# Attention and two token mixers on one core: the exponentials turned chunk by chunk, the value products of a pair issued together, and a planner with other prices

## The chip, the core and the metric

The kernel runs on one core of a Trainium2 chip. The metric is device time in microseconds (us) of one execution, the median of several runs. TensorE (PE in the profile) multiplies matrices, VectorE (DVE), ScalarE (ACT) and GpSimd (POOL) work on elements, and the queue of SyncE (SP) issues the transfers.

## The reference, cut to what matters

```
q_n, k_n = rmsnorm(q, g_q), rmsnorm(k, g_k)        # q, k, v: 4 x 12 heads x 448 x 64
scores = scale * q_n @ k_n^T ; scores -= max       # 448 x 448 for each head
attn = exp(scores) / (sum + 1e-9)
x = concat(attn @ v)                               # 4 x 448 x 768
h = relu(x @ w_in); u, v = halves of h             # first mixer (gated over tokens)
x = (u * (w_spatial @ norm(v) + b)) @ w_out
u = x + (relu(x^T @ w_tok1) @ w_tok2)^T            # second mixer, over tokens
out = u + relu(u @ w_ch1) @ w_ch2                  # and over channels
```

## The kernel before

48 heads are worked as 24 pairs; a pair's two heads lie side by side on the 128 partitions. The first eight pairs (`WHOLE`) multiply queries and keys in plain fp32; later ones split each operand into two fp32r parts and make three passes. Up to pair 9 (`AFTER`) the division by the softmax sum follows the value product; from pair 10 on POOL scales the exponentials first (`normalise`).

A pair's 448 queries are four chunks of 112. For a chunk, `scores` makes two score tiles (one for each head, both at once in half the array's rows each: 64 rows by 128 columns), DVE takes the negated row maxima (`nm`), and ACT the exponentials (`e`, 112 x 896 for both heads, ring of six). The value product needs the exponentials with the keys on the partitions, so `turned` transposes them on PE into PSUM (`tp`) and ACT or DVE copies them out (`et`). There are seven key tiles to a pair. Before, `turned(i, n)` takes one key tile out of all four chunks: four transposes of 112 columns and one copy of 128 x 448, into a ring of six `et` tiles. Five of seven copies are ACT's and two (`ON_DVE`) are DVE's. `values(i, kc)` multiplies one of four groups of keys with the values, the two heads in half the array's columns each (128 rows by 64 columns), and accumulates in one bank (`av`).

`slot(s)` writes the work of pair s's scores among the turning and the value products of pair s - 1, and `merge` weaves that with the first mixer (`moe`, one generator for each batch of six pairs) and the conversion of the weights. None of that is the final order. Every operation goes into a `Plan`: `estimate` gives it a price in ns, and `place` simulates the engines by list scheduling, eight rounds backward and forward, and keeps the shortest. Three of its parts matter here. An operation is marked by `op.parts` if it uses half of the array; the plan adds `SWITCH` ns to a matmul whose mark differs from that of the one before, and looks among what is ready (within `NEAR`) for work of the same mark first. Half-array matmuls that belong together are joined and stay next to each other. A pool's ring (`bufs`) makes the first writer of a buffer wait for all users of the tile that held it. `sync` (SP) is an engine of the plan like the others, so the order of the transfers comes out of it too.

The program after the first mixer (second mixer over tokens, then over channels, a Strassen form) is planned by the same code and has no half-array work.

Of the kernel before, what the change touches and what calls it, by code (L numbers as in the profile page):

```python
# [149 lines left out]
class Plan:  # L150
# [8 lines left out]
    def add(self, engine, fn, args, kwargs):  # L159
# [17 lines left out]
        op.parts = engine == "tensor" and fn == "matmul" and (ins[0].shape[0] <= 64 or out.shape[0] <= 64)  # L177
# [9 lines left out]
        for x in ins:  # L187
            t = x.tile
            assert t.writers, "read before it is written"
            op.deps.update(w for y, w in t.writers if x.meets(y))  # L190
# [23 lines left out]
    def estimate(self, engine, fn, out, ins, kwargs):  # L214
# [4 lines left out]
        if engine == "tensor":  # L219
# [27 lines left out]
    def fence(self, pools, act):  # L247

        op = Op()
        op.engine, op.call, op.cost, op.late, op.more, op.parts = "fence", act, 0, 0, [], False  # L250
# [12 lines left out]
    def place(self, before, after, lag, weight, tiles=None):  # L263
# [9 lines left out]
        parts, port = False, 0.0  # L273
# [151 lines left out]
SWITCH, NEAR = 75, 2500  # L425
# [6 lines left out]
TO = {"tensor": 100, "scalar": 0, "vector": 0, "gpsimd": 28, "sync": 0, "fence": 0}  # L432

# [17 lines left out]
def attention_moe_mixer(  # L451
# [150 lines left out]
    class Attention:  # L602
# [88 lines left out]
        def scores(self, i, c):  # L691
# [3 lines left out]
            if c == 0:  # L695
                self.sums[i] = p.tile([P, 2 * C], F32, tag="sum", bufs=3, name="sums")
            sums, qt, kt = self.sums[i], self.qt[i], self.kt[i]
            nm = p.tile([P, 2], F32, tag="nm", bufs=4, name="nm")
            e = p.tile([T, 2, S], F32, tag="e", bufs=6, name="e")
            sc = [psum.tile([P, 512], "sc", "sc")[:T, :S] for _ in range(2)]  # L700
            cs = slice(c * T, (c + 1) * T)
            with nc.joined_up():
                for n, (x, w) in enumerate(PASSES[:1] if i < WHOLE else PASSES):
                    for r in range(2):
                        me = slice(r * D, (r + 1) * D)
                        if i < WHOLE:
                            nc.tensor.matmul(sc[r], qt[me, cs], kt[me], start=True, stop=True)
                        else:
                            nc.tensor.matmul(
                                sc[r], qt[me, x, cs], kt[me, w], start=n == 0, stop=n == len(PASSES) - 1)  # L710
            for r in range(2):
                nc.vector.reduce_max(nm[:T, r:r + 1], sc[r], axis=AX.X, negate=True)
            for r in range(2):
                at = 2 * c + r
                nc.scalar.activation(
                    e[:, r], sc[r], AF.Exp, bias=nm[:T, r:r + 1], scale=1.0, accum_out=sums[:T, at:at + 1])
            self.e[i, c] = e
# [31 lines left out]
        def turned(self, i, n):  # L749
# [10 lines left out]
            tpf = tp.rearrange("p c t -> p (c t)")  # L760
            if n in ON_DVE:
                nc.vector.tensor_copy(et, tpf)
            else:
                nc.scalar.activation(et, tpf, AF.Copy)

        def values(self, i, kc):
# [4 lines left out]
            if kc == 0:  # L771
# [674 lines left out]
```

## Time and profile before

| | |
|---|---|
| time, median of 3 runs (range) | 909.92 us (909.79 to 911.64) |
| the profiled execution's own time; its span | 912.7 us; 910.2 us |
| mean granted TensorE clock | 0.996 |
| busy: PE, DVE, ACT, POOL | 872.9 (96%), 691.1 (76%), 532.3 (58%), 421.5 (46%) us |
| instructions: PE, DVE, ACT, POOL | 5134, 1335, 1267, 533 |
| chain that ended last, share of the span | PE 78%, DVE 7%, ACT 6%, DMA 4%, issue 2% |

Busy time is the time in which an engine had work by the profile, and the share is of the span. The time of an execution is 2.5 us over its span here. The attention with the first mixer takes about the first half of the span. All operations have one line in the profile (that of the recording layer), so groups are told apart by the names of their tiles. A matmul of plain fp32 with half of the array leaves two records in the trace, so a `values` group (two instructions in the order) is four records, and so is a `scores` chunk of the first eight pairs; a chunk of a later pair is six instructions and six records.

### The profile page before, as it was taken

The page shows a single profiled execution, that of the slowest core. Times are in us where ns is not written, and L with a number is a line of the kernel's source. Part 1 is how long each engine was busy: PE and PEld are TensorE (multiplying, and loading weights), DVE is VectorE, ACT ScalarE, POOL GpSimd, SP SyncE. Part 2 cuts the span into 40 slices and gives each one's busy share as a digit, 9 for nine tenths or more (in the row PEclk, how much of TensorE's full clock was granted, in tenths as well). Part 3 has the DMA queues.
Part 4 walks back from the last instruction along what each step waited for, and adds up shares of the span by engine and source line. Part 5 has one row for each costly group of instructions (what it writes and reads, how often), then busy time and mean ns, then how long its engine had stood idle before and what let it go on. Part 6 is the DMA issues. An engine that isn't in the chain of part 4 may idle for free.

```text
span 910.2 us, 15803 instructions
## 1 busy us (share of the span) xinstructions
PE 872.9 (96%) x5134; PEld 713.2 (78%) x5134; DVE 691.1 (76%) x1335; ACT 532.3 (58%) x1267; POOL 421.5 (46%) x533
## 2 busy tenths in 40 slices
PE   3889999999999999999999999999999999999998
PEld 1444476777677677767888999988898999999998
DVE  4799889776786766887555336777799997899973
ACT  5998987777776766776443446645325655333331
POOL 2665655776576555455224313466600307334550
PEclk9999999999999999999999999999999999999999
DMA  6555655566534666344678657766563874661441
GB/s 155 152 140 155 192 141 140 157 209 176 169 88 123 175 192 188 83 132 126 199 250 266 206 160 248 264 175 198 154 179 90 245 225 153 198 191 47 137 156 62
DMA packets 149106, 152.30 MB, mean 167 GB/s; under 512 B 77856, under 2 KB 130656, under 8 KB 147488
## 3 DMA queue, kind: packets, MB, share of 16 engines
q1 hardware_dynamic: 149024, 151.29, 56.1%
q8 instruction: 41, 0.67, 0.3%
q14 instruction: 41, 0.34, 0.1%
HBM read 112.44 MB, written 38.80 MB: 166 GB/s over the span
## 4 chain that ended last, share of the span: by engine, by line
PE 78%; DVE 7%; ACT 6%; DMA 4%; issue 2%; SPq 1%; POOL 1%; ACTq 0%; DVEq 0%; POOLq 0%
PE o_ps L418 15%; PE h2ps L418 15%; PE tp L418 8%; PE av L418 6%; PE ups L418 6%; PE vps L418 6%; PE sc L418 5%; PE xps L418 5%; PE sps L418 4%; ACT e L418 3%; PE u_ps L418 3%; PE h1ps L418 3%; SPq L418 1%; DVE word L418 1%; DMA c_d<-word 1%
## 5 line engine op out<-in xcount | busy, mean ns | idle before, releaser
L418 PE MATMUL h2ps<-op,w 128*128 128x448 f32 x756 | 157.6, 369 | 1.0 <-DVE c L418 1.0
L418 PE MATMUL o_ps<-w,op 128*128 128x384 f32 x882 | 154.0, 335 | 2.7 <-ACT w L418 1.4
L418 PEld LDWEIGHTS o_ps<-w,op 128*128 128x128 f32 x882 | 152.8, 188 | 3.8 <-ACT w L418 1.7
L418 PEld LDWEIGHTS h2ps<-op,w 128*128 128x128 f32 x756 | 142.3, 189 | 15.1 <-DVE c L418 2.4
L418 ACT ACTIVATE e<-sc,nm 112x448 f32<-112x448 f32 x192 | 120.5, 636 | 36.5 <-DVE nm L418 18.9
L418 DVE TENSOR_REDUCE nm<-sc 112x1 f32<-112x448 f32 x192 | 110.3, 616 | 16.6 <-PE sc L418 15.8
L418 POOL TENSOR_TENSOR src<-src 128x384 f32<-128x384 f32 x48 | 61.3, 1288 | 102.3 <-DMA src<-c_d 94.8
L418 PE MATMUL tp<-ident,e 112*128 112x112 f32 x672 | 95.0, 262 | 5.0 <-ACT et L418 2.2
L418 PEld LDWEIGHTS tp<-ident,e 112*128 112x128 f32 x672 | 74.3, 140 | 25.6 <-ACT et L418 7.0
L418 ACT ACTIVATE op<-c 128x768 fp32r<-128x768 f32 x49 | 41.5, 847 | 84.8 <-PE o_ps L418 67.8
L418 POOL TENSOR_SCALAR e<-e,sums 112x448 f32<-112x448 f32 x112 | 71.9, 658 | 38.6 <-DVE sums L418 14.5
L418 ACT ACTIVATE et<-tp 128x448 f32<-128x448 f32 x120 | 65.1, 550 | 22.2 <-PE tp L418 19.9
L418 DVE TENSOR_SCALAR word<-word 128x256 uint32<-128x256 uint32 (+5 forms) x132 | 58.2, 456 | 25.7 <-ACT word L418 24.6
L418 DVE SCALAR_TENSOR_TENSOR word<-raw,word 128x256 uint32<-128x256 uint32 (+2 forms) x132 | 74.1, 567 | 1.1
L418 PE MATMUL ups<-xp,wu 128*128 128x448 f32 x288 | 70.4, 379 | 0.0
L418 POOL TENSOR_TENSOR u<-u,o 128x384 f32<-128x384 f32 x28 | 41.1, 1480 | 62.9 <-ACT o L418 34.2
L418 PE MATMUL av<-et,v 128*64 128x448 f32 x288 | 65.9, 557 | 0.1
L418 DVE TENSOR_TENSOR op<-c,op 128x768 fp32r<-128x768 f32 x49 | 57.6, 1176 | 9.5 <-ACT op L418 9.3
L418 PE MATMUL xps<-wo,g 128*128 128x256 f32 x432 | 62.2, 290 | 1.2 <-DVE sums L418 0.8
L418 DVE TENSOR_TENSOR w<-src,w 128x384 fp32r<-128x384 f32 x84 | 60.0, 737 | 3.4 <-ACT w L418 3.4
L418 DVE TENSOR_TENSOR c<-c,h2ps 128x448 f32<-128x448 f32 x84 | 49.7, 616 | 14.0 <-PE h2ps L418 13.7
L418 PEld LDWEIGHTS xps<-wo,g 128*128 128x128 f32 x432 | 55.1, 190 | 6.6 <-issue 1.3
(120 smaller groups left out, 1653.5 us busy)
## 6 DMA issues: line engine op xcount, KB each, us to landing
src<-c_d SPq DMA_DIRECT2D x132, 192.0 KB, 2.8
wu<-wu_d SPq DMA_DIRECT2D x16, 768.0 KB, 4.8
wo<-wo_d SPq DMA_DIRECT2D x12, 1024.0 KB, 5.1
raw<-in_moe_w_ch_dram SPq DMA_DIRECT2D x36, 256.0 KB, 3.4
raw<-in_moe_w_ch_dram SPq DMA_DIRECT2D x24, 384.0 KB, 3.8
raw<-in_q_dram SPq DMA_DIRECT2D x48, 112.0 KB, 3.0
u<-u_d SPq DMA_DIRECT2D x28, 192.0 KB, 3.8
out_dram<-u SPq DMA_DIRECT2D x28, 192.0 KB, 2.1
```

The lines of the kernel that those rows point to most:

```text
L418: getattr(getattr(self.nc, op.engine), fn)(*args, **kwargs)
```

## The change

`turned(i, c)` now takes one chunk through all seven key tiles: seven transposes into two PSUM tiles (four and three), and two copies, 128 x 4 x 112 and 128 x 3 x 112, into one `et` tile for the pair (`bufs=1`). DVE copies the smaller half of chunks 1 and 3. `values(i)` issues the four groups of a pair in one call. In `slot`, chunks 0 and 1 of pair s are turned within its own slot, chunks 2 and 3 in the next, and `normalise(s, 2)` stands at the slot's end. The ring of `e` goes from six to five. In the planner half-array work has two marks (1: half the rows; 2: half the columns), `SWITCH` goes from 75 to 200 ns, and the prices of half-array matmuls are lower. `covered` only checks that a tile is written before it is read.

```diff
-        op.parts = engine == "tensor" and fn == "matmul" and (ins[0].shape[0] <= 64 or out.shape[0] <= 64)
+        op.parts = 0
+        if engine == "tensor" and fn == "matmul":
+            op.parts = 1 if ins[0].shape[0] <= 64 else 2 if out.shape[0] <= 64 else 0
...
-                return 0.326 * n if ins[0].shape[0] <= 64 else n / 2.4 + 13, 200
-            if ins[0].shape[0] <= 64:
-                return 1.04 * n, 200
-            return n / 1.2 + 54 if out.shape[0] <= 64 else n / 0.6, 200
+                return 0.223 * n if ins[0].shape[0] <= 64 else n / 2.4 + 15, 200
+            return 0.838 * n if min(ins[0].shape[0], out.shape[0]) <= 64 else n / 0.6, 200
...
-SWITCH, NEAR = 75, 2500
+SWITCH, NEAR = 200, 2500
...
-        def turned(self, i, n):
+        def turned(self, i, c):
...
-            r, kc = n % 2, n // 2
-            t = kc * P + r * (S + R)
-            tp = psum.tile([P, C, T], "tp", "tp")
-            for c in range(C):
-                nc.tensor.transpose(
-                    tp[:, c, :], self.e[i, c].rearrange("p r k -> p (r k)")[:, t:t + P], ident[:T, :T])
-            et = self.et[i, n] = self.p.tile([P, S], F32, tag="et", bufs=6, name="et")
+            if c == 0:
+                self.et[i] = self.p.tile([P, ET, S], F32, tag="et", bufs=1, name="et")
+            e = self.e[i, c].rearrange("p r k -> p (r k)")
+            for h, tiles in enumerate((range(C), range(C, ET))):
+                tp = psum.tile([P, C, T], "tp", "tp")
+                for n in tiles:
+                    t = n // 2 * P + n % 2 * (S + R)
+                    nc.tensor.transpose(tp[:, n - tiles[0], :], e[:, t:t + P], ident[:T, :T])
+                et = self.et[i][:, tiles[0]:tiles[-1] + 1, c * T:(c + 1) * T]
+                tpf = tp[:, :len(tiles)]
+                if (c, h) in ON_DVE:
+                    nc.vector.tensor_copy(et, tpf)
+                else:
+                    nc.scalar.activation(et, tpf, AF.Copy)
...
-        def values(self, i, kc):
+        def values(self, i):
...
+            for kc in range(C):
+                with nc.joined_up():
+                    for r in range(2):
...
-    ON_DVE = (3, 5)
-    SLOT = 10
-    PREP0, LAG, SPAN = 1, 0.5, 6
+    ET, EB = 2 * C - 1, 5
+    ON_DVE = (1, 1), (3, 1)
+    SLOT = 8
+    TWO = 99
+    PREP0, LAG, SPAN = 1, 0.2, 5.8
```

The statements of `slot` in their new order:

```
load(s+2) load_v(s) scale(s+1) scores(s,0) | turned(s-1,2) | turned(s-1,3) transposed(s+1,0) |
scores(s,1) normalise(s,0) transposed(s+1,1) values(s-1) | scores(s,2) | turned(s,0) norms(s+2) |
turned(s,1) | scores(s,3) normalise(s,2)
```

What the plan makes of it differs on every engine nearly from the start; only the last 1,627 of PE's instructions (the channel mixer, but for its first few matmuls) stand as before. Three places follow.

PE around the value product of pair 14 (its values' tile is v_3435 before and v_3437 after; `sc` are score matmuls, `av` the value product, `sps` and `ups` the first mixer's). Before:

```order
L418 MATMUL sc<-kt,qt 112x448 x6
L418 MATMUL av<-et,v_3435 64x448 x2
L418 MATMUL sps<-ws,vn 128x448 x3
L418 MATMUL tp<-ident,e 128x112 x7
L418 MATMUL sps<-ws,vn 128x448 x4
L418 MATMUL tp<-ident,e 128x112
L418 MATMUL sps<-ws,vn 128x448
L418 MATMUL tp<-ident,e 128x112 x3
L418 MATMUL sps<-ws,vn 128x448
L418 MATMUL tp<-ident,e 128x112
L418 MATMUL av<-et,v_3435 64x448 x4
L418 MATMUL av<-et,vrest 64x448 x2
```

After, PE for the same pair:

```order
L419 MATMUL sc<-kt,qt 112x448 x12
L419 MATMUL ups<-xp,wu 128x448
L419 MATMUL av<-et,v_3437 64x448 x6
L419 MATMUL av<-et,vrest 64x448 x2
L419 MATMUL sc<-kt,qt 112x448 x12
L419 MATMUL sps<-ws,vn 128x448 x2
L419 MATMUL tp<-ident,e 128x112 x7
L419 MATMUL sps<-ws,vn 128x448 x8
L419 MATMUL tp<-ident,e 128x112 x7
```

The four groups of the value product stand in one piece, score chunks by twos, and a chunk's seven transposes together.

SP's queue at the start (`raw` are the queries and keys of pairs 0 and 1, `g` the two gain vectors, loaded by four transfers). Before, from its sixth row on:

```order
L418 DMA g<-in_g_q_dram 64x1
L418 DMA g<-in_g_k_dram 64x1
L418 DMA g<-in_g_q_dram 64x1
L418 DMA raw<-in_q_dram 112x4x64 x2
L418 DMA raw<-in_k_dram 112x4x64
L418 DMA g<-in_g_k_dram 64x1
L418 DMA raw<-in_k_dram 64x64
L418 DMA raw<-in_k_dram 112x3x64
L418 DMA raw<-in_k_dram 48x64
```

After, SP from the same place:

```order
L419 DMA raw<-in_q_dram 112x4x64 x2
L419 DMA raw<-in_k_dram 112x4x64
L419 DMA raw<-in_k_dram 64x64
L419 DMA raw<-in_k_dram 112x3x64
L419 DMA raw<-in_k_dram 48x64
L419 DMA g<-in_g_q_dram 64x1
L419 DMA g<-in_g_k_dram 64x1
L419 DMA g<-in_g_q_dram 64x1
L419 DMA g<-in_g_k_dram 64x1
```

The last gain transfer stands behind three more transfers than before.

ACT at the start (`whole` are the transposed queries and keys of a pair, `e` its exponentials, `word` and `wpart` weights that are converted). Before, from the copies of pair 0 to those of pair 1:

```order
L418 ACTIVATE whole<-tp,gg 128x448
L418 ACTIVATE word<-raw 128x512
L418 ACTIVATE ry<-ra 112x16
L418 ACTIVATE ry<-ry 112x16
L418 ACTIVATE e,sums<-sc,nm 112x448 x4
L418 ACTIVATE word<-raw 128x512
L418 ACTIVATE sq<-raw 112x512
L418 ACTIVATE e,sums<-sc,nm 112x448 x2
L418 ACTIVATE sq<-raw 112x512
L418 ACTIVATE e,sums<-sc,nm 112x448 x2
L418 ACTIVATE whole<-tp 128x448
L418 ACTIVATE whole<-tp,gg 128x448
```

After, ACT over the same stretch and on to the first copies of `et`:

```order
L419 ACTIVATE whole<-tp,gg 128x448
L419 ACTIVATE word<-raw 128x512 x2
L419 ACTIVATE e,sums<-sc,nm 112x448 x4
L419 ACTIVATE whole<-tp 128x448
L419 ACTIVATE whole<-tp,gg 128x448
L419 ACTIVATE e,sums<-sc,nm 112x448 x4
L419 ACTIVATE et<-tp 128x4x112
L419 ACTIVATE et<-tp 128x3x112
```

Pair 1's copies stand four exponentials earlier, and pair 0's first chunk is copied out right behind its exponentials.

## Rows read from the trace of the kernel before

**Rows 1.** Windows: stretch, length, each engine's busy us (instructions), PE clock, DMA share, GB/s.

```profile
50.00:100.00 50.00, 44.93 (x271) 21.85 (x268) 45.50 (x96) 46.25 (x129) 29.11 (x42) 1.00 0.53 148
130.00:480.00 350.00, 346.90 (x2211) 257.57 (x2210) 257.42 (x615) 235.81 (x638) 192.57 (x303) 1.00 0.55 160
```

**Rows 2.** Timeline of PE, 184 to 201 us: start, time, operation, records.

```profile
184.04 2.39 PE L418 MATMUL sps<-ws,vn 128*128 128x448 f32 x11
186.27 0.55 PE L418 MATMUL tp<-ident,e 112*128 112x112 f32 x4
...
187.58 1.47 PE L418 MATMUL sc<-kt,qt 64*112 64x448 f32 x12
188.98 0.88 PE L418 MATMUL ups<-xp,wu 128*128 128x448 f32 x3
...
192.77 0.55 PE L418 MATMUL tp<-ident,e 112*128 112x112 f32 x4
193.25 0.97 PE L418 MATMUL av<-et,v 128*64 128x448 f32 x4
194.15 0.47 PE L418 MATMUL sps<-ws,vn 128*128 128x448 f32 x1
194.46 0.45 PE L418 MATMUL tp<-ident,e 112*128 112x112 f32 x3
...
197.67 0.93 PE L418 MATMUL tp<-ident,e 112*128 112x112 f32 x8
198.53 1.72 PE L418 MATMUL av<-et,v 128*64 128x448 f32 x8
200.19 0.86 PE L418 MATMUL sc<-kt,qt 64*112 64x448 f32 x6
200.97 0.97 PE L418 MATMUL av<-et,vrest 128*64 128x448 f32 x4
```

**Rows 3.** ACT's groups by form: busy us, mean ns of one, idle before.

```profile
L418 ACT ACTIVATE et<-tp 128x448 f32<-128x448 f32 x120 | 65.1, 550 | 22.2 <-PE tp L418 19.9 <-PE av L418 1.9
...
L418 ACT ACTIVATE ws<-tp 128x336 fp32r<-128x336 f32 x4 | 1.9, 464 | 0.7 <-PE tp L418 0.7
```

**Rows 4.** DVE's groups by form.

```profile
L418 DVE TENSOR_REDUCE nm<-sc 112x1 f32<-112x448 f32 x192 | 110.3, 616 | 16.6 <-PE sc L418 15.8
...
L418 DVE COPY et<-tp 128x448 f32<-128x448 f32 x48 | 29.8, 621 | 21.1 <-PE tp L418 20.9
...
L418 DVE TENSOR_TENSOR ws<-tp,ws 128x336 fp32r<-128x336 f32 x4 | 2.0, 492 | 0.0
```

**Rows 5.** Timeline of SP's queue, 7 to 10 us: start, issue time, transfer.

```profile
7.48 0.50 SPq L418 DMA_DIRECT2D g<-in_g_k_dram  x1
8.02 1.74 SPq L418 DMA_DIRECT2D raw<-in_k_dram  x3
```

**Rows 6.** Timeline of DVE at the start; in brackets the idle time before and its releaser.

```profile
9.84 0.27 DVE L418 TENSOR_TENSOR gg<-g 128x1 f32<-128x1 f32 x1 [2.85 <-DMA g<-in_g_k_dram]
...
10.23 0.69 DVE L418 TENSOR_TENSOR raw<-raw,ry 112x512 f32<-112x512 f32 x1
```

**Rows 7.** Timeline of PE at the start.

```profile
10.97 1.75 PE L418 MATMUL tp<-ident,raw 112*128 112x112 f32 x8 [10.97 <-DVE raw L418]
...
19.43 1.01 PE L418 MATMUL sc<-whole 64*112 64x448 f32 x4
24.26 3.20 PE L418 MATMUL sc<-whole 64*112 64x448 f32 x8 [3.82 <-ACT whole L418]
```

**Rows 8.** Windows around PE's pause in the third ten microseconds.

```profile
20.60:24.20 3.60, 0.00 (x0) 0.00 (x0) 3.56 (x9) 3.60 (x13) 0.73 (x2) 0.94 0.75 176
24.20:27.50 3.30, 3.24 (x9) 1.19 (x10) 1.16 (x3) 2.60 (x10) 2.35 (x6) 0.55 0.46 122
```

**Rows 9.** POOL's groups by form.

```profile
L418 POOL TENSOR_SCALAR e<-e,sums 112x448 f32<-112x448 f32 x112 | 71.9, 658 | 38.6 <-DVE sums L418 14.5 <-ACT sq L418 8.5 <-PE sc L418 4.9
```

More of the change, by code (lines that the diff above doesn't have):

```diff
@@ L189, in add @@
             assert t.writers, "read before it is written"
+            assert t.make or covered(x, t.writers), "read before all of it is written"
             op.deps.update(w for y, w in t.writers if x.meets(y))
@@ L249, in fence @@
         op = Op()
-        op.engine, op.call, op.cost, op.late, op.more, op.parts = "fence", act, 0, 0, [], False
+        op.engine, op.call, op.cost, op.late, op.more, op.parts = "fence", act, 0, 0, [], 0
         op.port = False
@@ L272, in place @@
         start = [0.0] * len(ops)
[L273 removed]
+        parts, port = 0, 0.0
         bank = {}
@@ L432, with covered, volume @@
 TO = {"tensor": 100, "scalar": 0, "vector": 0, "gpsimd": 28, "sync": 0, "fence": 0}
+def covered(x, writers):
+    left = volume(x.box)
+    for y, _ in writers:
+        left -= volume([(max(a, c), min(b, d)) for (a, b), (c, d) in zip(x.box, y.box)])
+    return left <= 0
+def volume(box):
+    n = 1
+    for a, b in box:
+        n *= max(0, b - a)
+    return n
 def free(shape):
@@ L689, in transposed, with scores @@
                 self.raw.pop(i), self.r.pop(i)
-        def scores(self, i, c):
+        def scores(self, i, *cs):
             if not 0 <= i < NP:
@@ L694, in scores @@
             p = self.p
-            if c == 0:
+            if cs[0] == 0:
                 self.sums[i] = p.tile([P, 2 * C], F32, tag="sum", bufs=3, name="sums")
             sums, qt, kt = self.sums[i], self.qt[i], self.kt[i]
[L698 to L701, printed above, removed]
+            scs = {c: [psum.tile([P, 512], "sc", "sc")[:T, :S] for _ in range(2)] for c in cs}
@@ L702, in scores @@
             with nc.joined_up():
[L703 to L717, printed above, removed]
+                for c in cs:
+                    sc, at0 = scs[c], slice(c * T, (c + 1) * T)
+                    for n, (x, w) in enumerate(PASSES[:1] if i < WHOLE else PASSES):
+                        for r in range(2):
+                            me = slice(r * D, (r + 1) * D)
+                            if i < WHOLE:
+                                nc.tensor.matmul(sc[r], qt[me, at0], kt[me], start=True, stop=True)
+                            else:
+                                nc.tensor.matmul(
+                                    sc[r], qt[me, x, at0], kt[me, w], start=n == 0, stop=n == len(PASSES) - 1)
@@ new lines, in scores @@
+            for c in cs:
+                nm = p.tile([P, 2], F32, tag="nm", bufs=4, name="nm")
+                e = self.e[i, c] = p.tile([T, 2, S], F32, tag="e", bufs=EB, name="e")
+                for r in range(2):
+                    nc.vector.reduce_max(nm[:T, r:r + 1], scs[c][r], axis=AX.X, negate=True)
+                for r in range(2):
+                    at = 2 * c + r
+                    nc.scalar.activation(
+                        e[:, r], scs[c][r], AF.Exp, bias=nm[:T, r:r + 1], scale=1.0, accum_out=sums[:T, at:at + 1])
@@ L770, in values @@
             b, j = divmod(i, KD)
[L771 to L773 removed]
+            av = mm_tile("av")
             v32, rest = self.v32[i]
[L775 to L782 removed]
+            for kc in range(C):
+                with nc.joined_up():
+                    for r in range(2):
+                        lhs = v32[:, r, kc] if kc < C - 1 else rest[:, r]
+                        rhs = self.et[i][:, 2 * kc + r if kc < C - 1 else 2 * kc]
+                        nc.tensor.matmul(
+                            av[r * D:(r + 1) * D, :S], lhs, rhs, start=kc == 0, stop=kc == C - 1)
             at = i % XB
@@ L830, in slot @@
             yield
-            self.turned(s - 1, 0)
-            self.turned(s - 1, 1)
+            self.turned(s - 1, 2)
             yield
-            self.values(s - 1, 0)
+            self.turned(s - 1, 3)
             self.transposed(s + 1, 0)
```

37 lines of the change are left out of this document (8 added, 29 removed).

## The prediction

> **What bounds the kernel now.** I read the page's busy shares first, then windows by stage, then PE's timeline, then what ACT, DVE and SP do at the start. From 130 to 480 us, the stretch in which attention and the first mixer run together, PE is busy 346.90 of 350 us at full clock while ACT has 236 and DVE 257 [rows 1]: there the time is PE's own, and a microsecond less of PE work is a microsecond less of span. From 50 to 100 us, where only attention and the conversion of weights run, PE, DVE and ACT are all near 90% (44.9, 45.5 and 46.3 of 50) [rows 1]: a triangle in which a saving on one engine need not show. Behind 480 us nothing of the change is left but what the plan shuffles; the last 1,627 matmuls keep their order, and I count that part at nothing (half a microsecond either way).
>
> **What a visit to half of the array costs.** PE's timeline gives the price of each step as the distance between starts [rows 2]. One group of the value product (four records) takes 0.90 us until the next operation starts (193.25 to 194.15), two groups 1.66 (198.53 to 200.19): 0.76 a group and 0.14 for a visit. A score chunk (six records) takes 0.78 (200.19 to 200.97), two chunks 1.40 (187.58 to 188.98): 0.62 a chunk and 0.16 a visit. The neighbours pay too. Eight transposes ahead of a value product take 0.86, four take 0.48: 0.095 each, so four should take 0.38 and the passage into the half array adds 0.10. The first full-array matmul behind the value product takes 0.31 (194.15 to 194.46) where eleven take 2.23, or 0.20 each (184.04 to 186.27): 0.11 for the passage out. I use 0.105 for either.
>
> **The sum on PE.** The multiplications stay the same in number and shape: as many transposes, score and value matmuls. What changes is how often PE goes from one form to another. Counted along the two orders, stretches of value products go from 60 to 32 (24 pairs, so before a pair's four groups came in two or three pieces), stretches of score chunks from 71 to 58, and passages between half and full array, both directions together, from 144 to 150, since score and value stretches that used to lean on each other are now more often apart. 28 x 0.14 = 3.9 less, 13 x 0.16 = 2.1 less, 6 x 0.105 = 0.6 more: 5.4 us less. Of the changes of form, 66 become 58 up to the value product of the sixth pair, and 137 become 107 behind it, so some nine tenths of the saving lie where PE sets the time.
>
> The Trainium skill (TensorEngine Tiling (Array Packing), Key Properties) says that changing the tiling mode, and not just the tile, drains TensorE, so by it every one of the 203 changes of form before, 165 after, would cost alike. At the mean of the rows' costs (60 x 0.14 + 71 x 0.16 + 144 x 0.105 = 34.9 us over 203, 0.17 each) the sum by that rule would be 38 x 0.17 = 6.5 us, one more than by the rows; the trace agrees that the direct passage from scores to values costs too, which the old plan took for none.
>
> **Copies out of PSUM.** A pair had seven copies of 448 columns, five on ACT at 550 ns [rows 3] and two on DVE at 621 [rows 4]. It gets four of 448 and two of 336 on ACT, two of 336 on DVE. The trace has 336 columns out of PSUM at 464 ns on ACT [rows 3] and at 492 on DVE (a subtraction, not a copy) [rows 4]. ACT: 4 x 550 + 2 x 464 - 5 x 550 = 378 ns more a pair; DVE: 2 x 492 - 2 x 621 = 258 less. Behind 130 us both engines have a fourth of their time free, so this hides. In the first eight pairs ACT gains 3.0 us of work and DVE loses 2.1. Bounds: 0 if the balance of the three engines takes it up, 3.0 if ACT alone sets the pace. I take 1.0, the net of both, being nearest to a stage in which they are equally full.
>
> **The start.** DVE begins pair 0's scaling only behind the product of the gains, which waits for the fourth gain transfer until 9.84 [rows 6]; PE's first work waits for that scaling at 10.97 [rows 7]. The fourth gain was issued at 7.48, and three issues of keys took 1.74 behind it [rows 5]. Now those three stand ahead of it, and DVE's queue still has the product ahead of the scaling: 1.7 us later, for PE and everything after it. Against it: pair 1's copies out of PSUM stood behind eight exponentials and now behind four. Before, PE paused 3.82 us for them at 20.4 and came back slow: eight records of scores took 3.20 us at 24.26, where four had taken 1.01 [rows 7], because the granted clock was 0.55 of full there (near the lower of its two levels) [rows 8]. In the pause ACT was busy 3.60 of 3.60 and DVE 3.56 [rows 8], so the pause itself was covered; what was lost is the slow stretch behind it, 3.20 - 2.02 = 1.2, and ACT's and DVE's idle time in it (0.7 and 2.1 of 3.3) [rows 8]. Bounds for the whole start: 1.7 slower if nothing is won back, 2.5 faster if the slow stretch goes and the idle time of ACT and DVE is used. I take 1.0 faster than without it for the slow stretch, so 0.7 slower, and 0.9 us of saved passages in the early stage is not counted at full. Start, copies and that stage come to about 1 us slower, and what mixer work comes earlier to fill PE's pauses (the first mixer's first matmul stands 7 us of PE work earlier in the order, into a stage that is a tenth idle: 0.7) brings it to nothing. I count the first 130 us at 0, bounds -5 and +5.
>
> **The sum.** The profiled execution took 912.7 us (span 910.2), 2.8 over the median of 909.92. 912.7 - 5.4 + 0 = 907.3; as a median 904.5.
>
> **New waits.** The pair's one `et` tile makes a pair's first copy wait for the last value matmul of the pair before; behind that copy in ACT's queue stand exponentials and other copies. In PE's order the next transposes come behind the value product nearly everywhere, so the wait is mostly over by then. The ring of five `e` tiles holds one chunk back until four chunks earlier is turned, which is long done. From pair 10 on, the chunk's turning waits for POOL's scaling: two maxima at 616 ns [rows 4] for each of two chunks, the exponentials, then two or four scalings at 658 ns [rows 9]. Before, the first two chunks of a pair had plenty of PE work in between (8 us at least, counted at the prices above) and the last two some 5; now both have from 5 up. PE waited little for either before (346.90 busy of 350), so I take 0 with a bound of 0.5 a pair, 7 us for 14 pairs.
>
> **Rivals.**
> First, faster than that: turning a chunk right behind its exponentials shortens the way through the first six pairs. PE idles 5.07 of 50 us in that stage [rows 1], 9.4 over the 92 us from 21 to 113; if half of it goes, 4.7 us more: 899.8. For it: chunks no longer wait for the pair's fourth exponential. Against: ACT has 92% of its time full there and gets more.
> Second, no change: the scaling on POOL arrives late at both halves of a pair. 14 pairs at 0.35 us are 4.9, and 909.4 is left. For it: the two halves are now equally tight. Against: the last two chunks were as tight before, and PE hardly waited.
> Third, slower: the one `et` tile stops ACT. A whole value product takes 0.14 + 4 x 0.76 = 3.2 us, and if ACT stands for a third of it (1.1) in each of the first eight pairs, where nothing makes up for it, that is 8.5; with 1.7 at the start and 1.0 of copies, less 5.4, 5.8 us more: 915.7. It decides from 0.35 us a pair on. Against it is the order: copies stand behind value products.
> That the plan would not bring the groups together is ruled out by the order itself.
>
> **How the numbers follow.** The forecast has 0.56, its own range 900.5 to 908.5; the faster case 0.19; no change 0.12; slower 0.13. About 0.2% (1.8 us) is what a measurement of this kernel tells from no change: faster means below 908.1, slower above 911.7. The forecast gives 0.53 faster and 0.03 same; the faster case all of its 0.19; the second 0.02, 0.09 and 0.01; the third all slower but for 0.01. Together 0.74, 0.13, 0.13. The range goes from 897 (start at its good bound on top of most of the first rival) to 911.5, leaving out most of the slow case.
>
> **What would show it.** Right: from 130 us on PE's busy time stays at its level while the first mixer ends some 5 us earlier; a value product of four groups takes about 3.2 us in one piece; the copies take about 465 ns for 336 columns on ACT; PE's first transposes start at about 12.6. Wrong: `av` or `et` as releaser of ACT's waits by more than 3 us in the first 120 us; PE waiting for POOL's `e` in several pairs; the stage behind 600 us longer by more than a microsecond; or a visit whose cost did not go although the stretches were joined.

## The result, and the profile after

The changed kernel takes 900.49 us (median of four runs, 898.39 to 902.25) against 909.96 for the kernel before on the same chip: 0.9877 of its time, 95% interval 0.9854 to 0.9900. The profiled execution took 900.49 us against 912.7, its span 898.7 against 910.2. Forecast were 904.5: the direction was right and the time lay in the range, but a gain of 5.4 us was forecast, and 9.5 (by the medians) to 12.2 (by the profiled executions) were measured. The gain was mis-sized by about a factor of two.

Windows of the changed kernel, columns as in [rows 1]; the first two answer to [rows 8], the next two to [rows 1]:

```profile
20.60:24.20 3.60, 3.40 (x22) 1.63 (x20) 3.60 (x8) 3.31 (x11) 0.00 (x0) 1.00 0.64 162
24.20:27.50 3.30, 2.11 (x17) 1.46 (x15) 3.30 (x9) 3.30 (x9) 1.84 (x2) 1.00 0.47 118
50.00:100.00 50.00, 44.67 (x273) 23.90 (x269) 42.72 (x100) 47.49 (x136) 35.53 (x50) 0.97 0.57 161
130.00:480.00 350.00, 344.90 (x2239) 265.03 (x2239) 254.36 (x633) 243.98 (x666) 198.85 (x304) 1.00 0.59 174
```

Where PE stood idle for 3.60 us it now works 3.40, and the granted clock stays at 1.00, the higher level. The lower level comes once later instead: from 53.8 to 57.2 us, behind a pause of 0.96 us (the 0.97 of the third row). From 130 to 480 us PE is busy 2.0 us less than before (344.90 of 350 against 346.90) and still starts 2,239 records where it started 2,211: more work in the same stretch. The stage that changed most is in neither row. Windows from 100 to 130 us, first of the kernel before:

```profile
100.00:130.00 30.00, 28.64 (x167) 16.73 (x166) 25.86 (x62) 25.33 (x74) 17.05 (x27) 1.00 0.59 161
```

The changed kernel:

```profile
100.00:130.00 30.00, 30.00 (x175) 19.66 (x173) 25.08 (x63) 25.11 (x70) 17.92 (x28) 1.00 0.54 150
```

**How the gain is placed.** Busy time hides the cost of passages, so I counted useful work: each matmul that starts before a time t, at the distance of its starts in long undisturbed runs of its form (0.203 us for `ups` and `sps`, 0.096 for a transpose, 0.755 for a `values` group). The sum for the changed kernel less that for the one before is its lead at t: -1.1 us at 20, +1.2 at 30, +2.0 at 100, +5.6 at 130, +10.8 at 480, +11.4 at 850. So 5.6 us come from the first 130 us, 5.2 from the next 350, and 0.6 from the rest. This splits the 11.5 us between the spans of the two profiled executions; the medians lie 9.5 apart, so some 2 us of it is scatter between executions.

**The sixth pair** shows what happens before 130 us. The first mixer's products take the value products of six pairs: its first few matmuls can run on the pairs that are done, but no product is complete before the sixth. PE's timeline (start, time, operation, records), score and value products of that pair and the mixer's first matmul, in the kernel before:

```profile
84.29 1.01 PE L418 MATMUL sc<-whole 64*112 64x448 f32 x4
...
98.38 0.97 PE L418 MATMUL av<-et,v 128*64 128x448 f32 x4
...
105.33 1.01 PE L418 MATMUL av<-et,v 128*64 128x448 f32 x4
...
109.03 0.97 PE L418 MATMUL av<-et,vrest 128*64 128x448 f32 x4
...
115.63 0.73 PE L418 MATMUL vps<-wv,xp 128*128 128x512 f32 x2
```

The same in the changed kernel, with the first rows of the start, which answer to [rows 7]:

```profile
12.29 1.75 PE L419 MATMUL tp<-ident,raw 112*128 112x112 f32 x8 [12.29 <-DVE raw L419]
14.81 3.33 PE L419 MATMUL sc<-whole 64*112 64x448 f32 x8 [0.76 <-ACT whole L419]
...
20.79 1.01 PE L419 MATMUL sc<-whole 64*112 64x448 f32 x4
21.73 0.89 PE L419 MATMUL tp<-ident,e 112*128 112x112 f32 x7
22.82 1.76 PE L419 MATMUL sc<-whole 64*112 64x448 f32 x8 [0.20 <-ACT e L419]
...
82.25 1.01 PE L419 MATMUL sc<-whole 64*112 64x448 f32 x4
...
100.03 2.48 PE L419 MATMUL av<-et,v 128*64 128x448 f32 x12
102.33 0.92 PE L419 MATMUL av<-et,vrest 128*64 128x448 f32 x4
103.94 1.40 PE L419 MATMUL vps<-wv,xp 128*128 128x512 f32 x5
```

The last score chunk of the sixth pair comes 2.0 us earlier, its last value group 6.7 earlier, the mixer's first matmul 11.7 earlier. From last score chunk to last value group (starts; I call it the lag) it was 24.7 us and is 20.1; the mean over the first six pairs fell from 21.7 to 17.4.

The start answers to [rows 5, 6]. SP's queue (start, issue time, transfer):

```profile
4.97 2.17 SPq L419 DMA_DIRECT2D raw<-in_k_dram  x4
...
8.99 0.59 SPq L419 DMA_DIRECT2D g<-in_g_k_dram  x1
```

and DVE:

```profile
11.41 0.16 DVE L419 TENSOR_TENSOR gg<-g 128x1 f32<-128x1 f32 x1 [2.94 <-DMA g<-in_g_k_dram]
11.54 0.69 DVE L419 TENSOR_TENSOR raw<-raw,ry 112x512 f32<-112x512 f32 x1
```

The copies, by form, answer to [rows 3, 4] (busy, mean ns, idle before). ACT's:

```profile
L419 ACT ACTIVATE et<-tp 128x448 f32<-128x448 f32 x96 | 53.1, 553 | 8.0 <-PE tp L419 7.3 <-PE av L419 0.2
L419 ACT ACTIVATE et<-tp 128x336 f32<-128x336 f32 x48 | 22.1, 460 | 2.2 <-PE tp L419 2.2
```

DVE's:

```profile
L419 DVE COPY et<-tp 128x336 f32<-128x336 f32 x48 | 24.2, 503 | 19.7 <-PE tp L419 19.6
```

### The profile page after: what moved, and what is told of

Same layout as the page of the kernel before. It is cut to its first block, busy times and chain, and to the rows that moved or that the text cites. A ratio compares the mean times of both kernels' runs of the same rounds, so it can differ in the third digit from the quotient of the medians.

```text
span 898.7 us, 15829 instructions
## 1 busy us (share of the span) xinstructions
PE 862.1 (96%) x5134; PEld 716.5 (80%) x5134; DVE 674.8 (75%) x1335; ACT 537.3 (60%) x1291; POOL 426.7 (47%) x533
## 4 chain that ended last, share of the span: by engine, by line
PE 72%; DVE 12%; ACT 8%; DMA 3%; issue 2%; SPq 1%; POOL 1%; ACTq 0%; DVEq 0%
PE h2ps L419 14%; PE o_ps L419 12%; PE tp L419 8%; PE av L419 6%; PE ups L419 6%; PE xps L419 5%; PE sc L419 5%; PE vps L419 4%; PE sps L419 4%; PE u_ps L419 3%; PE h1ps L419 3%; ACT e L419 3%; DVE c L419 3%; DVE op L419 2%; DVE w L419 2%
## 5 line engine op out<-in xcount | busy, mean ns | idle before, releaser
L419 POOL TENSOR_TENSOR src<-src 128x384 f32<-128x384 f32 x48 | 56.5, 1187 | 103.8 <-DMA src<-c_d 90.1
L419 PE MATMUL tp<-ident,e 112*128 112x112 f32 x672 | 90.4, 264 | 6.4 <-ACT et L419 4.1
L419 POOL TENSOR_SCALAR e<-e,sums 112x448 f32<-112x448 f32 x112 | 73.7, 678 | 23.8 <-DVE sums L419 7.8
L419 ACT ACTIVATE et<-tp 128x448 f32<-128x448 f32 (+1 forms) x144 | 70.4, 522 | 10.2 <-PE tp L419 9.5
L419 POOL TENSOR_TENSOR u<-u,o 128x384 f32<-128x384 f32 x28 | 43.5, 1570 | 57.6 <-ACT o L419 32.2
L419 DVE TENSOR_SCALAR word<-word 128x256 f32<-128x256 f32 (+5 forms) x132 | 50.4, 387 | 25.5 <-ACT word L419 24.9
L419 DVE TENSOR_TENSOR op<-c,op 128x768 fp32r<-128x768 f32 x49 | 54.9, 1121 | 9.3 <-ACT op L419 9.2
L419 PE MATMUL av<-et,v 128*64 128x448 f32 x288 | 60.1, 549 | 1.4 <-ACT xo L419 1.4
```

The source lines that it names most:

```text
L419: getattr(getattr(self.nc, op.engine), fn)(*args, **kwargs)
```

## The experiments

One table first. Own slot: which chunks are turned in their pair's own slot (in brackets: turning by key tile, as before). Sixth: start of its last value group. Mixer: the first mixer's first matmul. Lead: useful work ahead of the kernel before at 130 us, and what is added from 130 to 480 and from 480 to 850. Passages: us of passages and visits, at the prediction's prices, fewer behind the sixth pair along the order than before (23.3). Ratio: time over that of the kernel before on the same chip. All columns from lag to passages are read from one profiled execution of each kernel, while the time is a median: executions of one kernel lie up to 9 us apart (e9, 904.55 to 913.19). e3, e5 and e6, whose other edit spoiled the stage from 130 us on (leads there fell by 17.8, 19.8 and 7.8), are left out; their lags are 22.1, 22.6 and 22.1, their leads at 130 us -0.7, +1.1 and -2.4.

| kernel | own slot | lag | sixth | mixer | lead at 130 | to 480 | to 850 | passages | us | ratio |
|---|---|---|---|---|---|---|---|---|---|---|
| before | (none) | 21.7 | 109.0 | 115.6 | 0 | 0 | 0 | 0 | 909.96 | 1 |
| changed | 0, 1 | 17.4 | 102.3 | 103.9 | +5.6 | +5.2 | +0.6 | 4.4 | 900.49 | 0.9877 |
| e1 | (none) | 21.5 | 109.9 | 120.6 | -3.4 | -1.3 | -1.5 | -0.3 | 915.47 | 1.0033 |
| e2 | 0, 1 | 17.4 | 102.8 | 101.1 | +6.2 | +0.8 | -2.2 | 5.1 | 908.87 | 0.9971 |
| e4 | 0, 1 | 18.1 | 104.1 | 105.4 | +3.6 | -2.6 | +7.5 | -9.1 | 903.52 | 0.9900 |
| e7 | 0, 1 | 17.3 | 100.7 | 102.8 | +6.7 | +5.1 | +6.2 | 5.0 | 894.19 | 0.9811 |
| e8 | 0, 1 | 17.3 | 103.6 | 104.8 | +3.8 | +8.9 | +2.5 | 7.9 | 897.10 | 0.9851 |
| e9 | none | 20.6 | 110.3 | 111.2 | -0.7 | +6.5 | -4.2 | 5.4 | 907.38 | 0.9957 |
| e10 | 0 | 19.9 | 109.4 | 110.9 | -3.1 | +7.5 | +3.4 | 5.7 | 903.34 | 0.9899 |
| e11 | 0, 1 | 17.2 | 101.5 | 103.1 | +6.9 | +6.4 | +3.0 | 7.2 | 896.10 | 0.9829 |
| e12 | 0, 1 | 18.3 | 104.3 | 107.8 | +2.1 | +8.6 | +1.2 | 7.9 | 898.51 | 0.9855 |
| e13 | 0, 1, 2 | 17.9 | 102.0 | 103.5 | +6.1 | +1.6 | +7.2 | 5.3 | 897.20 | 0.9837 |
| e14 | 0, 1, 2 | 17.5 | 99.2 | 100.8 | +8.8 | +4.8 | +1.6 | 4.1 | 895.27 | 0.9804 |

**Prices alone (e1), and the change with the old prices (e2).** e1 is the kernel before with the planner's part of the change, e2 the changed kernel without it:

```diff
-SWITCH, NEAR = 75, 2500
+SWITCH, NEAR = 200, 2500
```

(e1; with it the two marks and the lower prices; e2 takes all three back.)

> The kernel before with the planner's new prices, its two marks for half-array work and SWITCH = 200, and nothing else of the change. Theory (structure): of the 11 us gained, some 5 are passages between forms of the array, most of them after 130 us, and some 6 come in the first 110 us because ACT no longer waits for a free tile of exponentials (a chunk's tile is free after its own seven transposes, where all four chunks were held until the last key tile). The prices do neither: counted along this order, visits and passages cost 35.7 us against 34.9 before, and key tiles are still turned across all chunks. So 910 us, give or take 3, with the sixth pair's value product at 109 us as before. Rival (plan): the better prices make a shorter plan everywhere; then about 901 us, the sixth pair at 102 to 104.

> The changed kernel with the old prices, the one mark and SWITCH = 75. Theory (structure): the gain stays; visits and passages cost 29.2 us along this order against 29.5 in the changed kernel, chunks are turned one by one; 900 us, give or take 3, the sixth pair's value product at 102 us, give or take 2. Rival (plan): most of the gain goes, 906 to 910, the sixth pair at 106 or later.

e1: 1.0033, interval 1.0018 to 1.0048: the new prices gain nothing on the old order of work. e2: 0.9971 (0.9954 to 0.9987), 9 us over the forecast centre, so that forecast missed. Its lead at 130 us is the changed kernel's (+6.2): the early gain is not the prices'. Behind 130 us it gained only 0.8 of the 5.1 us that its passages promised. PE is idle there for 6.3 us where it was 3.1 before:

```profile
130.00:480.00 350.00, 343.69 (x2214) 259.15 (x2213) 253.11 (x638) 242.65 (x662) 192.66 (x301) 1.00 0.59 174
```

That accounts for 3 of the 4; the rest is that its changes of form cost only 2.8 us less there (counted as at the end of the part on the passages below), not 5.1. Taken together, the changed kernel gained 1.2% and e2 gained 0.3%: the place of the work brings the early gain with either prices, but most of the time gained needs the new prices too, which bring nothing on the old order of work.

**A wider ring for the exponentials (e3).** Before, ACT's exponentials waited 4.5 us on transposes from 30 to 130 us, which still read the ring's tiles. Two more `e`, paid for with one of two buffers of weights (`wst`):

```diff
-            e = p.tile([T, 2, S], F32, tag="e", bufs=6, name="e")
+            e = p.tile([T, 2, S], F32, tag="e", bufs=8, name="e")
```

> The kernel before with eight tiles of exponentials for six (two whole pairs). To make room the first mixer's streamed weights have one buffer for two, which touches nothing before its second stage, so only the first 110 us are to be compared, not the whole time. Theory (ring): ACT's waits of exponentials for transposes, 4.5 us in the first 109 us before, go to under 1, and the sixth pair's value product ends at 103 to 106 us instead of 109. Rival (start): the early gain came from pair 1's copies standing earlier in ACT's queue, which removed PE's pause and the slow clock behind it; then the sixth pair stays at 108 to 110 here.

943.76 us, one run. The total says nothing, for the single weight buffer stopped PE (9.2 us for `wo`, from 130 to 480 us). The early stage can be read, if weakly: that wait fell to 0.3 us, yet the sixth pair came at 109.5 (109.0 before), where the theory had 103 to 106. The granted clock was 0.95 from 30 to 100 us (1.00 before), two stretches of 3.4 us at half, which cost 3.4 us at most. ACT waited for others instead. Its waits from 30 to 130 us in the kernel before (total, times, longest):

```profile
ACT e L418 <- PE tp L418: 4.5, 5, 1.8
...
ACT et L418 <- PE tp L418: 1.4, 3, 0.7
...
ACT e L418 <- DVE nm L418: 0.5, 1, 0.5
```

and in e3:

```profile
ACT xp L418 <- DVE over L418: 3.7, 3, 2.2
ACT et L418 <- PE tp L418: 3.6, 4, 1.6
ACT e L418 <- DVE nm L418: 2.4, 5, 0.8
```

**No grouping (e4).** `SWITCH, NEAR = 0, 0` in the changed kernel: the plan takes no care of form.

> The changed kernel with SWITCH = 0 and NEAR = 0: the planner no longer looks for work of the same form. Visits and passages along this order: 43 value stretches, 90 score stretches, 258 passages, by the prices read before 47.5 us against 29.5, of the 18.0 us more 13.5 behind the sixth pair. Theory: 13 to 18 us slower than the changed kernel, 913 to 919. Rival (passages hide behind other waits, and the 5.4 us were not the reason): within 4 us of the changed kernel, under 905.

903.52 us, 0.9900 (0.9872 to 0.9928): the total missed by ten. The number is the rival's (under 905). With 9.1 us more of passages behind the sixth pair than before, by the prices, it lost only 2.6 from 130 to 480 us. PE waited 1.4 us less, 1.7 us idle where it was 3.1, and its changes of form cost 4.7 us more, half of what the prices say. So the passages are paid, but these prices are too high for an order with many short visits.

```profile
130.00:480.00 350.00, 348.34 (x2208) 256.14 (x2207) 249.09 (x614) 243.71 (x663) 197.31 (x307) 1.00 0.56 164
```

And it gained 7.5 us behind 480 us, where the change has nothing to do: I take how the work falls there for chance of the plan.

**Value groups together, nothing else (e5); all chunks turned a slot later (e6, e9).** e5 puts the four groups into one call in the kernel before; e6 and e9 take the changed kernel and move the turning of chunks 0 and 1 into the next slot. What depends on the place moves along: the scaling of chunks 2 and 3 goes to the next slot, the value product from before the third score chunk to behind it. e5 and e6 got their room from the mixer's output tiles (`xo`, two to one); e9 keeps both and the ring of five.

```diff
-            self.turned(s - 1, 2)
-            yield
-            self.turned(s - 1, 3)
+            self.turned(s - 1, 0)
+            yield
+            self.turned(s - 1, 1)
...
+            self.turned(s - 1, 2)
             self.transposed(s + 1, 1)
+            yield
+            self.turned(s - 1, 3)
...
             self.values(s - 1)
...
-            self.turned(s, 0)
...
-            self.turned(s, 1)
```

> The kernel before with only the value groups of a pair in one call at the end of the slot (for that seven et tiles; the buffer that copies the first mixer's output has one place for two). Key tiles are still turned across all chunks. Visits and passages 31.8 us along this order against 34.9 before, of the 3.1 less 2.2 behind the sixth pair. Theory now (chunk by chunk turning brings the early gain, fewer passages a part of the later one): the sixth pair stays at 108 to 110 us, and from there to the last matmul of the first mixer it is 1 to 2 us shorter; 909 us in all, give or take 2. Rival (grouping the value product itself brings the early gain): sixth pair at 102 to 104 us, 903 in all.

> The changed kernel with all four chunks of a pair turned in the next slot, as before the change (six tiles of exponentials for that, one buffer for two for the first mixer's output). Chunks are still turned one by one, values still in one piece. Passages 27.6 us along this order against 29.5, 2.3 of it less in the first six pairs. Theory (spreading): chunk by chunk turning is quick because two chunks' copies fall among the pair's own exponentials, so ACT always has something ready; with all of them a slot later the sixth pair comes at 106 to 109 us and the whole at 905 to 908. Rival (form): one chunk through all key tiles is enough wherever it stands; sixth pair at 101 to 104, 900.

> The changed kernel with all four chunks of a pair turned in the slot of the next pair; ring of five e and two xo as in the changed kernel, so the last run of this question without its second edit. Passages between forms priced along the order: 26.6 us, fewer than the changed kernel's 29.5. If the early gain is the shorter way from a pair's scores to its value product: the lag over the first six pairs back at about 22 us (17.4 with the change, 21.7 before), the sixth pair's value product at 109 to 112 us, and the time at 904 to 909 with all passages saved all the same. If the turning by chunk and the joined value products bring the early gain by themselves: sixth pair at 102 to 104 and the time at 897 to 900.

e5 came to 1.0274 (1.0202 to 1.0345) and e6 to 1.0276 (1.0244 to 1.0309): PE's value product waited 6.0 and 3.4 us on the single `xo` from 130 to 480 us, a part of what they lost, so their totals say nothing. Their sixth pairs lie before that, at 110.9 and 111.6: grouping the value product alone brings no early gain, and with six tiles of `e` (e6) the late turning is no quicker. In e5 the mixer's first matmul started at 103.6, as early as with the change, and the lead at 130 us is only +1.1: what counts is when the sixth pair is through. e9 settles it: 0.9957 (0.9931 to 0.9983), sixth pair at 110.3, lead at 130 us -0.7. It keeps the turning by chunk, the joined value product, the copies, the prices and more than all of the later gain (+6.5); only the early gain is gone. Its lag came back to 20.6, three quarters of the way to that of the kernel before, and not, as expected, to 22. Windows of the first 130 us, in the kernel before:

```profile
0.00:130.00 130.00, 105.69 (x604) 54.79 (x605) 104.75 (x223) 108.38 (x297) 69.89 (x118) 0.99 0.59 157
```

in the changed kernel:

```profile
0.00:130.00 130.00, 109.18 (x633) 61.34 (x633) 100.56 (x228) 111.23 (x305) 73.11 (x120) 0.99 0.57 154
```

and in e9:

```profile
0.00:130.00 130.00, 103.85 (x589) 56.68 (x590) 98.80 (x218) 105.72 (x289) 63.45 (x115) 0.99 0.57 154
```

PE works 5.3 us less in e9 than in the changed kernel, which is most of the 6.3 us between their leads; 2.0 of the 6.3 are there at 30 us already. Each of the three has one stretch of 3.4 us at the lower clock (0.99 in all rows), so the clock does not set them apart. PE's timeline in e9, to be read beside the two above:

```profile
84.28 1.01 PE L419 MATMUL sc<-whole 64*112 64x448 f32 x4
...
102.41 0.79 PE L419 MATMUL tp<-ident,e 112*128 112x112 f32 x3 [0.97 <-ACT e L419]
103.13 1.84 PE L419 MATMUL sc<-whole 64*112 64x448 f32 x4
...
108.01 2.48 PE L419 MATMUL av<-et,v 128*64 128x448 f32 x12
110.32 0.92 PE L419 MATMUL av<-et,vrest 128*64 128x448 f32 x4
111.17 0.73 PE L419 MATMUL vps<-wv,xp 128*128 128x512 f32 x2
```

Scores as late as before, and the value product too; the mixer's first matmul comes 4.5 us sooner than before, without a lead.

**One chunk (e10) and three chunks (e13) in the own slot.** The same edit by degrees; in e13 `turned(s - 1, 2)` stands ahead of `scores(s, 0)`.

> The changed kernel with only chunk 0 turned in its pair's own slot, chunks 1 to 3 in the next. Passages 27.9 us. If the lag decides by degrees: lag 18.5 to 21, sixth pair between 103 and 109 us, time 899 to 906. If it is enough that anything at all is turned in the own slot: sixth pair at 102 to 103 as with the change. If the place of the turning does not matter: no difference from the run with all four a slot later, by less than 2 us at the sixth pair.

> The changed kernel with chunk 2 too turned ahead of the next pair's scores, so chunks 0 to 2 close to their exponentials and chunk 3 in the next slot. Passages 29.3 us, as with the change (29.5). If the lag from scores to value product is the cause of the early gain: lag over the first six pairs 14.5 to 17, sixth pair's value product at 98 to 103 us, useful PE work 4 to 9 us ahead of the kernel before at 130 us, time 895 to 901. If the even split of two and two is what counts: sixth pair at 105 to 110, ahead by 0 to 2 at 130 us, time 903 to 907.

e10: 0.9899 (0.9878 to 0.9920), 903.34 us as by degrees, but not for that reason: the early stage gained nothing (109.4, within a microsecond of e9; lead -3.1), and the time comes from behind 130 us. It does not decide the question, for one stop spoiled it. Two conversions of weights on DVE took 2.53 and 1.53 us where the median one takes 0.41, the maxima stood behind them, and ACT and PE waited:

```profile
53.08 3.98 DVE L419 TENSOR_SCALAR wpart<-wpart 128x256 f32<-128x256 f32 x2
```

```profile
59.45 1.57 PE L419 MATMUL tp<-ident,e 112*128 112x112 f32 x7 [3.27 <-ACT et L419]
```

The clock then stood at the lower level from 58.7 to 65.5 us, and the lead went from +0.4 at 55 us to -4.5 at 65. The sixth pair's own lag is 20.6, near the changed kernel's 20.1; it is its scores that come 6.6 us later. Whether one chunk gains a part stays open. e13: 0.9837 (0.9802 to 0.9871), sixth pair at 102.0, lead +6.1, as expected of the lag theory; the lag itself missed (17.9, expected 14.5 to 17): a third chunk shortens it no more. That the even split of two and two is what counts is ruled out. Over the table, the nine orders with a lag of 18.3 or less lead by 2.1 to 8.8 us at 130 us, and all with 19.9 or more by nothing or less (of those outside it, e5 leads by 1.1 with 22.6). The lag separates the two groups; within them it does not order the leads. From 130 to 480 us e13 gained 3.7 us less than its passages; PE's longest wait there is new (total, times, longest):

```profile
PE tp L419 <- ACT e L419: 2.8, 2, 2.1
```

**More room on ACT (e7), a wider search (e8), both (e11, e12), and e7 with three chunks (e14).** e7 gives all four copies of 336 columns to DVE, e8 lets the plan look 8000 ns ahead for work of the same form:

```diff
-    ON_DVE = (1, 1), (3, 1)
+    ON_DVE = (0, 1), (1, 1), (2, 1), (3, 1)
...
-SWITCH, NEAR = 200, 2500
+SWITCH, NEAR = 200, 8000
```

> The changed kernel with the copies of 336 columns of all four chunks on DVE, two of them moved from ACT. In its first 102 us ACT waited only at the start, so ACT's work sets the pace there: 2 x 482 ns less for each of six pairs is 5.8 us, DVE (76 of 102 us busy) gets 2 x 503 ns. Theory (ACT bounds the early stage): sixth pair at 97 to 100 us, 895 to 898 in all. Rival (latency through the chain bounds it): sixth pair at 101 to 104 us, 900.

> The changed kernel with NEAR = 8000 for 2500: the planner looks further for work of the same form. Visits and passages along this order 24.9 us against 29.5 (24 value stretches, 56 score stretches, 120 passages), 3.5 of the 4.6 less behind the sixth pair. Theory: from the sixth pair to the end of the first mixer 2 to 3.5 us shorter (in the run without grouping 13.5 us more in price were 7.9 in time there), 897 to 900 in all if the stage behind 530 us does not move; rival: work taken out of its turn makes others wait, and it is not shorter.

> The changed kernel with both edits that gained by themselves: all four copies of 336 columns on DVE, and the search for work of the same mark 8000 ns wide. Passages priced 25.9 us along the order, 29.5 with the change, so 3.6 less. If the two gains add (early lag and passages): sixth pair at 100 to 102 us, 889 to 894. If they are one gain, the same idle time filled twice: 894 to 898.

> The same with three of the four copies of 336 columns on DVE (chunks 0, 1 and 3). Passages priced 23.8 us, the fewest of these orders, 5.7 less than with the change. By passages alone 2 us under the kernel with four on DVE; by the early stage 0 to 1 over it: 889 to 895, sixth pair at 100.5 to 102.5 us. If the price of the passages is not what the stage from 130 us on pays, it comes out no better than the run with four on DVE alone (894).

> The same with all four copies of 336 columns on DVE. Passages 30.1 us. If the lag is the cause and ACT's room adds to it, as with two chunks in the own slot (894.2 against 900.5): sixth pair at 97 to 101 us, 889 to 895. If the even split counts: sixth pair at 103 to 108, 897 to 903.

e7: 894.19 us, 0.9811 (0.9781 to 0.9841), the fastest median. From 30 to 100 us ACT had been the fullest engine of the changed kernel:

```profile
30.00:100.00 70.00, 64.24 (x387) 33.68 (x387) 58.29 (x133) 67.50 (x192) 45.86 (x68) 0.98 0.57 159
```

In e7 it is level with DVE:

```profile
30.00:100.00 70.00, 64.32 (x397) 32.84 (x396) 66.29 (x143) 65.39 (x182) 43.25 (x67) 1.00 0.57 156
```

The sixth pair comes 1.6 us earlier, at 100.7, between the two forecasts. A part of that can be the clock, which is 0.98 in the first of these rows and 1.00 in the second. But e14 against e13, neither of them with a stretch at the lower clock before 130 us, shows 2.8 us for the same edit. Most of e7's advantage over the changed kernel (+5.6 of lead) arises behind 480 us. e8, 0.9851 (0.9816 to 0.9885), gained 8.9 us from 130 to 480, with 7.9 fewer of passages. e11 (0.9829, 0.9812 to 0.9845) has both gains at 480 us (+13.3) and ends behind e7 all the same; e12 (0.9855, 0.9835 to 0.9876) lost in the first 130 us what its fewer passages gave. By the leads at 480 us the two gains seem to add (the changed kernel +10.8, e7 +11.8, e8 +12.7, e11 +13.3), but the differences are no wider than the scatter; e11's time is that of the other forecast. e12 missed by 3.5 us and with its sixth pair (104.3). That it comes out no better than e7 was to speak against the price of the passages; from 130 to 480 us its lead grew by 8.6 all the same, for 7.9 saved. e14 (0.9804, 0.9761 to 0.9846) has the earliest sixth pair (99.2, as expected) and 895.27 us, 0.3 over its range. e7, e11 and e14 can't be told apart; each beats both kernels, their intervals lying clear of the changed kernel's.

## Why the prediction was wrong in size

**The step that failed** is "I count the first 130 us at 0, bounds -5 and +5". It measured +5.6, and with it the forecast would have been 899. (The 0.9 us of passages saved before the sixth pair were counted twice, in the 5.4 and in what brings the early stage to nothing; counted once, it is 900.) Its parts:

- **The start** was put at 0.7 us slower. The later gains cost as said: 8.99 against 7.48 for the last issue, 12.29 against 10.97 for PE's first work, 1.3 us instead of 1.7. But the pause was held to be "covered", since ACT and DVE were full in it [rows 8], and only the slow stretch behind it was credited. PE worked 3.40 of the 3.60 us there with ACT (3.31) and DVE (3.60) as full as before: they did other work first. At 30 us the lead is +1.2. That busy neighbours make a pause unavoidable does not follow; it depends on whether what PE waits for comes first in their queues.
- **The copies** were put at 1.0 us. Durations were right (460 ns for 464, 503 for 492), ACT's load from 30 to 100 us went from 64.34 to 67.50 of 70, and still the stage did not get slower (lead +0.8 over it). More room there still helps: the edit that takes 16 copies of 336 columns off ACT's first eight pairs brings the sixth pair 1.6 us sooner in e7, 2.8 in e14 against e13.
- **The mixer's earlier beginning** was put at 0.7 us: 7 us earlier into a stage that is a tenth idle. It came 11.7 us earlier, and the lead grew by 3.6 from 100 to 130 us: PE's idle 1.36 us went, its changes of form cost 1.2 us less (0.8 at the prediction's prices, 2.6 to 1.8), and the steps between full-array operations 0.7; the last 0.3 I can't place.

**The rival that was true** is the first, which had 0.19: "turning a chunk right behind its exponentials shortens the way through the first six pairs", with 899.8 us. e9 is its test: undo the place of two chunks, with what hangs on it, and 6.3 us of lead at 130 us are gone. The rival's size fits too: PE's idle time from 21 to 113 us fell from 11.4 to 7.8 us, 3.7 us where the rival had 4.7. That the whole time came out within a microsecond of its 899.8 is in part luck, since the terms behind 130 us moved as well. What spoke against it, that ACT has 92% of its time full and gets more, weighed too much: ACT was full, but what stood first in its queue was not always what the chain needed (at the start two `sq` of a later pair ahead of pair 1's copies).

**The passages were right for the change.** Forecast were 5.4 us, nine tenths of them behind the sixth pair; at its prices that part of the order has 4.4 less, which is eight tenths, and the lead grew by 5.2. A piece of PE's timeline after, to be read with [rows 2]:

```profile
192.58 0.50 PE L419 MATMUL xps<-wo,g 128*128 128x256 f32 x2
193.01 2.48 PE L419 MATMUL av<-et,v 128*64 128x448 f32 x12
195.42 0.39 PE L419 MATMUL xps<-wo,g 128*128 128x256 f32 x1
```

Three groups take 2.41 us to the next operation, 3 x 0.76 + 0.14 = 2.42 by the prediction's prices. Over nine of the twelve kernels of the table the lead from 130 to 480 us is within 2 us of the passages saved. It is not for e2, e4 and e13 (4.3 less, 6.5 more, 3.7 less). PE's idle time moved the other way there, but only by 3.2, 1.4 and 2.8 us. A direct count says more: take the distances between starts in half-array work and at the steps into and out of it, less idle time and less the undisturbed distances. From 130 to 480 us that sum is 5.1 us less in the changed kernel than before, 2.8 less in e2 and 4.7 more in e4; the prices have 4.4 and 5.1 less and 9.1 more. So they hold for the change and are too high for the orders of e2 and e4. In the changed kernel the steps between full-array operations cost 2.4 us less besides, which the prediction did not have, and 2.0 us of new idle time were lost again. Of the two sums weighed against each other there, 5.4 by the rows and 6.5 by one price for each change of form, the runs don't choose: the scatter of 2 us is wider than their difference.

**The new waits** were put at 0 with a bound of 7 us. The two that were feared did not come: from 130 to 480 us PE waited nowhere for POOL's `e`, and ACT's copies waited 0.2 us for `av` in the whole execution (the row of 448 columns above). But PE was idle 5.1 us there against 3.1, mostly behind ACT's copies of the mixer's output (`xo`), so 2.0 us of others did. The second and the third rival fall with that.

**The part behind 480 us** was put at nothing, "half a microsecond either way". It came to +0.6, but that was luck: over the table it runs from -4.2 to +7.5 for kernels whose code differs in the attention and in the planner's numbers alone, each read from one execution. PE's waits from 560 to 850 us in the changed kernel (total, times, longest):

```profile
PE h2ps L419 <- DVE c L419: 3.9, 3, 2.0
PE o_ps L419 <- DVE u L419: 2.2, 1, 2.2
```

and in e13, which gained 7.2 there:

```profile
PE o_ps L419 <- ACT op L419: 1.0, 1, 1.0
PE h2ps L419 <- DVE c L419: 0.6, 2, 0.4
```

The bounds for that term should have been 4 us and more on either side.

## What to carry to other kernels

Where a second phase can fill an engine's idle time, ask first when it may begin, and follow the chain that opens it (here scores, exponentials, transposes, value product of the sixth pair) before counting what an edit saves on the busy engine. A nearly full engine did not fix that chain's length here: what stood first in its queue counted as well as how much it had to do. And where one planner orders everything, a term of "nothing changes there" needs the bounds that other plans of the same work show.

## What the runs showed of the hardware

- The granted clock column says nothing of the first microseconds of PE's work. In the changed kernel the eight score records at 14.81 took 3.33 us and the eight at 22.82 took 1.76, and both stretches show a clock of 1.00 (14.80 to 18.00 us in the row below, 20.60 to 24.20 above). But this trace has no record of the clock before 19.67 us, and the column then stands at 1.00; which level the first eight ran at is not shown.

```profile
14.80:18.00 3.20, 3.19 (x8) 1.07 (x8) 2.18 (x3) 1.95 (x4) 2.68 (x5) 1.00 1.03 231
```

- A short pause can be followed by the lower level of the clock late in the stage too. In e9 PE waited 0.97 us at 101.4, and then four score records took 1.84 us instead of 1.01; the window shows 0.75. In the changed kernel the pause of 0.96 us before 53.70 was followed by the lower level in the same way, a pause of 1.19 us before 26.59 by none. The window of e9:

```profile
100.00:105.00 5.00, 3.81 (x19) 1.79 (x18) 3.90 (x12) 4.86 (x15) 1.11 (x3) 0.75 0.52 188
```
